# A fused attention and MLP kernel on one core: batch 0's set-up rebuilt, batch 1's inputs moved to GpSimd's DMA queue behind the weights

## The chip, the core and the metric

The kernel runs on one core of a Trainium2 chip. The metric is device time in microseconds (us). A core has a matrix engine (TensorE, PE in the profile), three other compute engines (VectorE or DVE, ScalarE or ACT, GpSimd or POOL) and SyncE (SP), which here only issues DMAs. Each engine executes its own instructions in program order and waits on semaphores for the others. PSUM is the memory that TensorE writes its results to.

Kernels sent in one call ran on the same chip and share the runs of the kernel before. The kernel before moved a little from call to call (medians 418.96 to 421.70 us), so between calls the ratios are compared, not the medians. A ratio is the mean time of one kernel's fast runs over that of the kernel before in the same rounds, so it is not quite the ratio of the quoted medians. Its 95% interval stands in brackets.

## The reference

Eight batches pass through windowed attention with eight global tokens, and then through a two-part MLP:

```python
# q, k, v: (8 batches, 8 heads, 576, 64); x after attention: (8, 576, 512)
scores = q @ k.T / 8, masked to |i-j| <= 32 or a global row or column (8 global tokens)
x   = softmax(scores) @ v
a1  = alpha1 * x + beta1
u   = x + lam * (w_tok @ a1)              # token mixing, w_tok is 576 x 576
ch  = relu((alpha2 * u + beta2) @ w_ch1) @ w_ch2     # 512 -> 2048 -> 512
out = u + lam * ch
```

## The kernel before

Names that return below: XL holds the scaled attention output that token mixing reads, UT the transposed u that the MLP reads, KTz a batch's transposed keys, wtT the transposed token weights, W1 and W2 the two MLP weights (each loaded in four blocks).

The rows of all batches are joined into nine MLP groups of 512 rows. While the MLP of one group runs, its matmuls are dealt out as "fillers" between the attention steps of the next batch, so that TensorE always has something to do. Batch 0 has no such partner, and batch 1 has only group 0.

```python
for _ in range(8): next(fill)             # fill yields after every MLP matmul
for b in range(1, NB):
    gen = front(b, kqn)                   # attention and mixing of batch b
    while True:
        try: n = next(gen)
        except StopIteration as s_: kqn = s_.value; break
        for _ in range(n): next(fill)
    done[0] = b + 1 if b < NB - 1 else 9  # groups below done[0] may run
for _ in fill: pass
```

For batches 0 and 1 the keys and queries are transposed on TensorE; batch 1's during batch 0's attention and mixing. From batch 2 on, `front(b)` loads the next batch's keys and queries on SyncE, casts them on GpSimd, and transposes them by DMA:

```python
# in front(b), when there is a batch b+1
cq = [qk_chunk(b + 1, c) for c in range(3)]         # loads on SyncE
kq, vg = gathers(b + 1)
yield from pg(b); yield from qk(b, 0)
for c in range(2): cq.pop(0)(G)                     # casts on GpSimd
for p in range(4):
    ...                                             # scores, global part
    pv(b, p, x)               # its last steps on GpSimd: XL[par] = x * (alpha1 * lam)
    if p == 0:   cq.pop(0)(G); cq = [qk_chunk(b + 1, c) for c in (3, 4)]
    elif p == 1: cq.pop(0)(G); cq.pop(0)(G)
    elif p == 2:
        kqn = glob_kq(kq)
        for c in range(5): xbar_k(c)                # DMA transposes on SyncE
        xbar_q()
        cv = [v_part(b + 1, i) for i in range(3)]   # V loads on SyncE
    else: ...                                       # V casts, shifts, global rows
yield 22
mix = tokmix(b, x)            # UT[g] = transpose of u*alpha2, by DMA on SyncE for b > 0
```

Each block of four output columns needs a bias row, which VectorE copies out of PSUM before ScalarE can apply relu:

```python
def mlp(g):
    for ec in range(16):
        if g == 0 and ec % 4 == 0: bias1(ec // 4)   # matmuls, then V.tensor_copy(bias1T)
        ps = ml()                                   # one of three PSUM buffers
        ... 4 matmuls into ps ...
        SC.activation(out=HTb[...], in_=ps, func=AF.Relu, bias=bias1T[:, ec:ec+1])
```

Batch 1's loads, and the issue of the weights, in program order (cut):

```python
n_k0 = qk4_half(1, 0, 0, next_r()); ...       # batch 1's k, q: SyncE, right after batch 0's
...
pv(0, 2, x); w1_dma(0); ...                   # W1 in four blocks on GpSimd
pv(0, 3, x); w1_dma(1); ...; w1_dma(2); w1_dma(3)
mix = tokmix(0, x) ...                        # batch 1's last key transposes in between
V.tensor_tensor(out=XL[1][0:1, 0, :], in0=b1r[0:1, :], in1=lamb[0:1, :], op=ALU.mult)
c_v = [v_part(1, i) for i in range(3)]        # batch 1's V: SyncE
for c in c_v: c(G)
v_shift(G)
for blk in range(4): w2_dma(blk)
```

The softmax here doesn't subtract the row's maximum and nothing guards it: scores larger than these inputs give would overflow.

## Time and profile before

The median of three runs was 417.88 us (417.57 to 422.43).

| event in the trace of before | us from start |
|---|---|
| first scores of batch 0 | 16.05 |
| first product with V (PV) | 22.8 |
| token mixing of batch 0 starts | 41.41 |
| first MLP matmul | 52.57 |
| second phase of MLP group 0 | 75.0 |
| token mixing of batch 1 | 87.3 |
| MLP group 1 starts | 108.20 |

From the page of the kernel before, these are the busy share of TensorE, its granted clock (10 tenths is printed as 9) and the DMA share, in forty slices of 10.4 us each, and then the chain that ended last:

```profile
PE   1665698969599999999999999999999999999995
PEclk9989999999699999999999999999999999999998
DMA  8996999999877999898999899899971003202001
PE 72%; DMA 12%; POOL 5%; DVE 4%; SPq 3%; issue 3%; ACT 1%; POOLq 0%; DVEq 0%
```

TensorE is full from the twelfth slice on. Only the first eleven slices, some 114 us, hold slack; the change is aimed at them. Each row of the next table is a stretch of the span (to the first MLP matmul, and from there to MLP group 1): length, then busy us of each engine, granted clock, DMA share and GB/s.

```profile
0.00:52.57 52.57, 28.91 (x393) 22.05 (x395) 36.97 (x92) 33.31 (x61) 32.34 (x51) 0.97 0.98 207
52.57:108.20 55.63, 45.40 (x435) 24.60 (x443) 29.63 (x61) 16.57 (x31) 31.05 (x40) 0.94 1.10 202
```

In the first stretch TensorE is busy 28.9 of 52.6 us, and in the second 45.4 of 55.6. TensorE's waits in the second stretch, as "who waited for whom: us in total, times, longest", are nearly two alone:

```profile
PE ml L482 <- DMA UT<-u_1502: 5.0, 1, 5.0
PE sc L401 <- POOL XL_116 L365: 3.2, 1, 3.2
```

### The profile page before, as it was taken

To read this page: it belongs to the slowest core of one execution; us is meant where nothing else is said; L and a number is where in the kernel's file an instruction comes from. 1 tells how busy PE (TensorE), PEld (TensorE's weight loads), DVE (VectorE), ACT (ScalarE), POOL (GpSimd) and SP (SyncE) were. 2 spreads that over 40 slices of the span, in tenths; PEclk is the share of its full clock that TensorE was granted. 3 is DMA by queue.
4 is the path that set the end of the run, shared out by engine and by line. 5 is a ranking of instruction groups with operands and counts; after the bars stand their busy time and mean duration, and the time that the engine had idled before them with its cause. 6 is when DMAs were issued, how large, how long until landed. Compare 5 with 4: busy or idle time off the path is not lost.

```text
span 415.1 us, 8399 instructions
## 1 busy us (share of the span) xinstructions
PE 372.6 (90%) x3349; PEld 206.5 (50%) x3403; DVE 227.2 (55%) x458; ACT 172.4 (42%) x303; POOL 181.1 (44%) x241
## 2 busy tenths in 40 slices
PE   1665698969599999999999999999999999999995
PEld 1554355524266456545654664466446644444442
DVE  6955843647246775575558753966374548114022
ACT  6848466300284047305730573047306720540720
POOL 7657354474445366754655473837440330000000
PEclk9989999999699999999999999999999999999998
DMA  8996999999877999898999899899971003202001
GB/s 235 224 301 105 171 218 193 210 161 244 190 138 115 194 219 215 148 209 186 212 151 206 196 211 170 175 222 192 166 178 53 2 27 85 56 0 77 25 25 76
DMA packets 174282, 64.14 MB, mean 155 GB/s; under 512 B 158498, under 2 KB 168226, under 8 KB 174244
## 3 DMA queue, kind: packets, MB, share of 16 engines
q1 hardware_dynamic: 167524, 54.63, 64.1%
q0 software_dynamic: 6720, 8.98, 11.7%
q8 instruction: 26, 0.43, 0.4%
q14 instruction: 12, 0.10, 0.1%
HBM read 39.28 MB, written 9.44 MB: 117 GB/s over the span
## 4 chain that ended last, share of the span: by engine, by line
PE 72%; DMA 12%; POOL 5%; DVE 4%; SPq 3%; issue 3%; ACT 1%; POOLq 0%; DVEq 0%
PE ml L491 26%; PE ml L482 26%; PE sc L405 6%; DMA vg<-in_v_dram,hg_idx 4%; PE xps L347 4%; DMA R_96<-in_v_dram 3%; PE sc L285 3%; PE xps L348 2%; DMA HTb<-in_moe_w_tok_dram 2%; PE mm L313 2%; SPq L203 1%; PE sc L330 1%; PE sc L401 1%; DMA RV_99<-in_v_dram 1%; POOL XL_116 L359 1%
## 5 line engine op out<-in xcount | busy, mean ns | idle before, releaser
L482 PE MATMUL ml<-UT,W_118 128*128 128x512 bf16 x542 | 141.0, 382 | 7.0 <-DMA UT<-u_1502 5.0
L491 PE MATMUL ml<-W_119,HTb 128*128 128x512 bf16 x561 | 135.2, 381 | 1.0 <-DMA W_119<-in_moe_w_ch_dram 0.2
L485 ACT ACTIVATE HTb<-ml,bias1T 128x512 bf16<-128x512 f32 x144 | 98.8, 688 | 87.8 <-PE ml L482 71.4
L491 PEld LDWEIGHTS <-HTb 128*128 128x128 bf16 x576 | 54.3, 98 | 61.3 <-issue 3.1
L482 PEld LDWEIGHTS <-W_118 128*128 128x128 bf16 x576 | 49.2, 99 | 45.9 <-issue 6.7
L496 DVE TENSOR_TENSOR tmp<-ml,lamb 128x512 f32<-128x512 f32 x36 | 24.8, 690 | 66.9 <-PE ml L491 50.8
L292 ACT ACTIVATE Pt<-sc 128x432 f16<-128x432 f32 x90 | 47.3, 528 | 14.2 <-PE sc L285 13.0
L285 PEld LDWEIGHTS <-KTz 128*128 128x128 bf16 x576 | 31.4, 102 | 21.3 <-PE mm L232 1.1
L359 POOL TENSOR_TENSOR XL_116<-x,LA_133 128x512 bf16<-128x512 f32 x16 | 20.8, 1300 | 32.6 <-DVE x L352 32.6
L285 PE MATMUL sc<-QT,KTz 128*128 128x72 bf16 x540 | 32.9, 200 | 1.1 <-DVE QT L235 0.8
L359 POOL TENSOR_TENSOR XL_115<-x,LA_133 128x512 bf16<-128x512 f32 x16 | 21.4, 1335 | 24.2 <-DVE x L352 23.2
L497 DVE TENSOR_TENSOR U<-tmp,U 128x512 f32<-128x512 f32 x36 | 29.5, 818 | 1.2
L406 DVE TENSOR_TENSOR U<-sc,x 128x512 f32<-128x512 f32 (+1 forms) x36 | 24.7, 687 | 9.1 <-PE sc L405 8.8
L331 ACT ACTIVATE GS_110<-sc 64x320 f16<-64x320 f32 (+1 forms) x8 | 3.2, 404 | 58.5 <-PE sc L330 58.2
L352 DVE TENSOR_TENSOR x<-xps,rden 128x640 f32<-128x640 f32 x32 | 26.4, 825 | 1.6
L331 ACT ACTIVATE GS_111<-sc 64x320 f16<-64x320 f32 (+1 forms) x8 | 3.2, 402 | 49.7 <-PE sc L330 49.7
L110 POOL CAST ve<-RV_98 128x1024 f16<-128x1024 f32 x8 | 10.0, 1244 | 31.4 <-DMA RV_98<-in_v_dram 31.3
L405 PE MATMUL sc<-XL_115,wtT_121 128*128 128x512 bf16 x79 | 19.7, 379 | 0.4 <-DVE U L406 0.3
L405 PE MATMUL sc<-XL_116,wtT_122 128*128 128x512 bf16 x76 | 19.7, 384 | 0.1
L294 DVE TENSOR_TENSOR GRT_108<-Pt,grm 128x80 f16<-128x80 f16 x16 | 4.3, 266 | 26.4 <-ACT Pt L292 26.4
L348 PE MATMUL xps<-RS_112,GS_110 128*128 128x65 f16 x160 | 15.9, 197 | 2.3 <-DVE RS_112 L321 2.3
L347 PEld LDWEIGHTS <-PTz_106 128*128 128x128 f16 x288 | 15.0, 97 | 5.8 <-DMA vo<-ve 1.6
(191 smaller groups left out, 525.1 us busy)
## 6 DMA issues: line engine op xcount, KB each, us to landing
out_dram<-U SPq DMA_DIRECT2D x36, 256.0 KB, 2.8
RV_99<-in_v_dram SPq DMA_DIRECT2D x16, 256.0 KB, 5.1
vo<-ve POOLq DMA_DIRECT2D x14, 260.0 KB, 4.1
R_97<-in_k_dram SPq DMA_DIRECT2D x12, 256.0 KB, 4.4
R_97<-in_q_dram SPq DMA_DIRECT2D x12, 256.0 KB, 5.3
RV_98<-in_v_dram SPq DMA_DIRECT2D x8, 256.0 KB, 3.9
W_118<-in_moe_w_ch_dram POOLq DMA_DIRECT2D x4, 512.0 KB, 8.9
W_119<-in_moe_w_ch_dram POOLq DMA_DIRECT2D x4, 512.0 KB, 13.7
```

Of the source, the lines that this page charges most:

```text
L285: T.matmul(out=ps[:, i * 144 + 72 * hh : i * 144 + 72 * hh + 72], lhsT=KTz[:, 2 * p + hh, 64 * t : 64 * t + P], rhs=A(QT, qo(t) + 80 * p, ...
L292: SC.activation(out=Pt[:, 432 * un : 432 * un + 432], in_=ps[:, 0:432], func=AF.Exp, bias=0.0, scale=0.125)
L347: T.matmul(out=o_, lhsT=ptz[:, base : base + P], rhs=vv, start=(i == 0), stop=False)
L352: V.tensor_tensor(out=A(x, P * p, [[64, 2], [DM, 5], [1, 64]]), in0=A(xps, 0, [[512, 2], [65, 5], [1, 64]]), in1=A(rden, 0, [[5, 2], [1, 5 ...
L359: G.tensor_tensor(out=A(xl, DM * full + P * p, [[DM, 4], [1, P]]), in0=A(x, DM * full + P * p, [[DM, 4], [1, P]]), in1=A(LA1, P * p, [[0, ...
L405: T.matmul(out=ps, lhsT=wtT[par][:, c, P * u : P * u + P], rhs=XL[par][:, c, :], start=(c == 0), stop=(c == 4))
L406: V.tensor_tensor(out=U[f][r0:r1, :], in0=ps[r0:r1, :], in1=x[r0:r1, u, :], op=ALU.add)
L482: T.matmul(out=ps, lhsT=W1[:, cc, ec * P : (ec + 1) * P], rhs=ut[:, cc, :], start=(cc == 0), stop=(cc == 3))
L485: SC.activation(out=HTb[:, slots[ec], :], in_=ps, func=AF.Relu, bias=bias1T[:, ec : ec + 1], scale=1.0)
L491: T.matmul(out=ps, lhsT=HTb[:, slots[ec], P * j : P * j + P], rhs=W2[:, ec, :], start=(ec == 0), stop=(ec == 15))
L496: V.tensor_tensor(out=tmp, in0=ps, in1=lamb, op=ALU.mult)
L497: V.tensor_tensor(out=u, in0=tmp, in1=u, op=ALU.add)
```

## The change

The intent is to shorten batch 0's start and to have every transfer arrive in the order in which it is needed. Core of the diff, with cuts:

```diff
-    def qk4_half(...) / qk4_rest(...)          # 4 heads per load, fixed to SyncE
+    def kq_load(E, b, i, h0, nh, r, off): ...   # any number of heads, engine E issues
+    onehot = cp.tile([P, 6, 8], BF16)           # global columns: keys x one-hot on TensorE
-    kq, vg = gathers(0)  ... gathers(1)         # for batches 0 and 1: indirect loads of k, q
+    vg = gather_v(0)     ... gather_v(1)        # only V is still gathered
+    def qk0_mm(p): ...                          # batch 0 scores on 64-row operands (XL[1] as buffer)
+    def v_half(hf, v4): ...                     # V of batch 0 in two halves; vo by copies
-    cq.pop(0)(G)                                # first two casts of batch b+1, for b >= 1
+    if cq and b > 1: cq.pop(0)(G)
-                if p == 0: ...  elif p == 1: ...  elif p == 2: ...  else: ...
+                late = b == 1                   # batch 2's casts and transposes one or two
+                if p == 2 * late: ...           # head pairs later than in other batches
+                elif p == 1 + 2 * late: ...
+                if p == 2 + late: ...           # DMA transposes, then V loads
+    wt_dma(0, 256); wt_dma(2, 256); wt_dma(4, 64); w1_dma(0)
     ... products with V of batch 0; w1_dma(1) between them ...
+    m3 = pv_mm(0, 3)
+    wt_tr(0); wt_tr(1)                          # token weights transposed after the last PV
+    w1_dma(2); w1_dma(3)
+    n_k = [kq_load(G, 1, 0, 4 * i, 4, R[i], 0) for i in range(2)]    # batch 1 on GpSimd
+    n_q = [kq_load(G, 1, 1, 0, 4, R[2], 0)]
+    n_rest = kq_rest(G, 1, u_tile())
+    n_q += [kq_load(G, 1, 1, 4 + 2 * i, 2, ub[i], 0) for i in range(2)]
+    c_v = [v_part(1, i, G, u_tile() if i == 2 else None) for i in range(3)]
     ... wt_tr, wt_sum ...
+    drain(tokmix(0, x))
+    G.memset(KTz, 0.0)                          # KTz no longer used by batch 0
+    G.memset(wtT[1][:, :, 0:64], 0.0); G.memset(wtT[1][0:64, 0, 64:640], 0.0)
+    for blk in range(2): w2_dma(blk)
+    G.memset(XL[1][0:64, 0, :], 0.0)            # XL[1] free only after batch 0's scores
     V.tensor_tensor(out=XL[1][0:1, 0, :], in0=b1r[0:1, :], in1=lamb[0:1, :], op=ALU.mult)
+    fillers(40)                                 # 40 MLP matmuls, then batch 1's transposes
+    for p in range(4): ... kt(1, p, V); fillers(3); qt(p, SC); fillers(3) ...
+    for blk in range(2, 4): w2_dma(blk)
     ...
-            for _ in range(n): next(fill)
+            fillers(n if b > 1 or used[0] < 64 else {4: 3, 5: 2, 6: 4, 10: 10}.get(n, 0))
```

## The prediction

> **What bounds the kernel now.** From about 112 us on the tensor engine (PE): its waits there sum to 1.1 us. Before that it is badly fed: the table by 5-us stretches shows 76 us of PE busy time in the first 110 us, so 34 us idle, and a granted clock of 0.66-0.67 at 25-30 and 90-95 us and 0.52 at 105-110 us. Only this part is changed. Landmarks in the timeline: scores of batch 0 begin at 16.05 us, PV at 22.8, token mixing at 41.4, the first MLP matmul at 52.6, MLP group 1 at 108.2. Large waits: 6.3 us for the first cast, 3.2 for XL at 87.7, 5.0 for the transposed u at 103.2. The chain of waits runs here through DMA: token weights (8.1 us), V of batch 1 (14.1), the V gather (14.6). Batch 1's q/k load from 19 us, ahead of W1, which is issued only at 37-43 us.
>
> **What the change does.**
> - Smaller first loads; no 2.19-us KTz memset and 2.33-us ScalarE copy before the first cast; batch 0's keys leave by one 128-row copy (about 0.7 us) instead of two 64-row ones (1.4 us).
> - One-hot columns remove k/q gathers (1 us of GpSimd each, plus landing) for batches 0 and 1, and add 80 small matmuls, at an estimated 0.06 us 2.4 us per batch.
> - V halves with on-chip shifts remove the vo transfer (4.5 us landing).
> - Batch 1 loads after the weights. The Trainium skill ("DMA: Bandwidth & Descriptors", Issuing engines are not separate DMA queues) says all queues share the same 16 engines; the trace agrees in that W1 blocks took 8.9 us (median) beside other loads. So order should help.
> - Batch 1's transposes move into MLP group 0; its attention gets fewer fillers (43 instead of 120), leaving 21 for batch 2.
>
> **On the critical path.** Estimates, from the new order with measured durations: scores near 10 us, PV near 20, XL complete near 32, mixing near 34, first MLP matmul 43-45. VectorE sets the pace (about 25 us of work before mixing, 8.4 us during it). That saves 8-9 us. From there to group 1 PE has about 47 us of work, including 4 us of moved transposes and one-hot products; I expect 5-9 us idle. The equivalent of group 1's start comes at 97-102 us instead of 108.2, and a re-throttle or two goes: the skill ("TensorE: Matmul & The Clock Gate", What's actually happening) says an idle window of about 3.4 us halves the clock; the trace has 0.52 around the 5.0-us wait. Net gain 6-15 us, centre 11.
>
> **Predicted: 407 us, 80% range 397 to 414. Faster by over 2%: 0.66; within 2%: 0.32; slower by over 2%: 0.02.**
>
> **What would show it.** First MLP matmul at 42-46 us; no 5-us wait for UT; PE idle in the first 100 us down by about 10 us; W1 block 0 landed before 40 us; batch 1's q/k/v landed by about 55 us.
>
> **What would make it wrong.** Smaller gain: GpSimd blocks on many small-row loads and a large KTz memset, so batch 1's keys come late; W2 blocks 2-3 late behind batch 1; three batch-2 casts ahead of batch 1's last XL product starve mixing by 3 us or more; VectorE sets batch 1's pace and the fewer fillers don't cover it. Larger gain: VectorE and DMA overlap better; the clock never drops from 40 to 110 us.

## The result and the profile after

The changed kernel took 442.19 us (440.75 to 444.42, four runs); the kernel before, beside it, 418.96 us (four runs). The ratio is 1.0546 [1.0462, 1.0630]: slower by 5.5%, where the centre of the prediction was faster.

| event | before, us | predicted, us | after, us |
|---|---|---|---|
| first scores | 16.05 | near 10 | 9.28 |
| first PV | 22.8 | near 20 | 24.0 |
| last XL product of batch 0 | | near 32 | 36.9 |
| token mixing starts | 41.41 | near 34 | 41.41 |
| first MLP matmul | 52.57 | 43 to 45 | 50.87 |
| as much left as at group 1 of before | 108.2 | 97 to 102 | 132.5 |

The last row is the span after, 439.3 us, less the 306.9 us that before still needed from its group 1 on (from the unrounded spans, 439.334 and 415.061 us). After's own group 1 starts at 134.50 us and needs 304.8 us. So nothing was lost behind group 1; the loss of 24.2 us between the two profiled spans lies ahead of it, and batch 0 even gave 1.7 us. The same rows of the page, after (slices of 11.0 us):

```profile
PE   3568728775967999999999999999999999999995
PEclk9985869999796999999999999999999999999999
DMA  7878999603999988998999898869995002301101
PE 70%; DVE 10%; DMA 7%; POOL 6%; SPq 3%; issue 3%; ACT 1%; DVEq 0%; POOLq 0%; ACTq 0%
```

Two things are new: the clock is lowest in the fourth and sixth slices, and the DMA engines are nearly idle in the ninth. The stretches after, cut at the first MLP matmul, the end of its long stall, batch 1's first attention matmul, its token mixing and group 1:

```profile
0.00:50.87 50.87, 31.03 (x409) 23.08 (x411) 36.76 (x95) 17.86 (x41) 34.49 (x50) 0.86 0.83 183
50.87:63.90 13.03, 4.07 (x12) 1.52 (x12) 0.75 (x2) 0.74 (x2) 11.17 (x11) 0.63 0.93 185
63.90:86.70 22.80, 17.96 (x174) 9.78 (x175) 10.70 (x25) 12.24 (x23) 7.05 (x8) 0.92 0.97 176
86.70:105.67 18.97, 15.45 (x256) 10.74 (x261) 14.73 (x32) 6.63 (x14) 7.95 (x9) 1.00 0.01 3
105.67:134.50 28.83, 18.87 (x99) 8.35 (x100) 12.77 (x21) 2.93 (x6) 14.12 (x21) 0.85 1.04 190
```

In the second row TensorE is busy for 4.1 of 13 us and VectorE and ScalarE for less than 1 each, while GpSimd is busy for 11.2. In the fourth row DMA moves 3 GB/s, and in the fifth it is full.

**The stall of 8.7 us.** GpSimd's timeline there, as "start, duration, engine, line, operation, what it writes and reads, count", with the idle time just before and what ended it in brackets:

```profile
46.42 0.83 POOL L209 DMA_DIRECT2D RV<-in_v_dram  x1 [3.07 <-DMA W<-in_moe_w_ch_dram]
48.64 0.90 POOL L209 DMA_DIRECT2D RV<-in_v_dram  x1 [1.39 <-DMA R<-in_k_dram]
50.90 0.88 POOL L209 DMA_DIRECT2D RV<-in_v_dram  x1 [1.37 <-DMA R<-in_k_dram]
53.28 0.88 POOL L209 DMA_DIRECT2D RV<-in_v_dram  x1 [1.50 <-DMA R<-in_q_dram]
...
55.10 4.38 POOL L813 MEMSET KTz<- 128x5120 bf16 x1
...
61.73 0.56 POOL L818 MEMSET XL<- 64x512 bf16 x1
```

A V load writes a free buffer and reads an input, so its data give it nothing to wait for. Yet each waits for another DMA to land. The operands in the trace show why: GpSimd's DMAs signal on eight completion semaphores, numbered 111 to 118, in turn, and each first waits until the DMA that had its semaphore before, the eighth back, has landed. The first V load waits on 118, which W1's last block had signalled; the next three wait on 111, 112 and 113, which belong to batch 1's two key loads and its first query load. These are exactly the releasers in the brackets, and the same count fits e1, e2, e5, e9 and e14 below. After four such waits (7.3 us) come the clear of KTz, two clears of wtT, two W2 issues, and only then the small clear of XL. VectorE, ScalarE and TensorE stood in line behind it:

```profile
62.33 0.68 DVE L823 TENSOR_TENSOR XL<-U,lamb 1x512 bf16<-1x512 f32 x1 [11.50 <-POOL XL L818]
62.94 0.14 DVE L579 COPY bias1T<-mm 128x4 f32<-128x4 f32 x1
63.16 1.84 ACT L557 ACTIVATE HTb<-ml,bias1T 128x512 bf16<-128x512 f32 x3 [21.27 <-DVE bias1T L579]
63.90 1.44 PE L554 MATMUL ml<-UT,W 128*128 128x512 bf16 x3 [8.73 <-ACT HTb L557]
```

VectorE writes one row of XL (L823), which needs the clear. It stands ahead of the bias copy, and VectorE runs in order. The relu lacks its bias, no PSUM buffer comes free, and TensorE, which could fill three, stops. The XL row itself is used more than 40 us later, in the mixing of batch 1 (105.67 us).

The Trainium skill ("TensorE: Matmul & The Clock Gate", What's actually happening) says that after an idle window of about 3.4 us TensorE falls back to half clock. The trace agrees: the wait lasted from 55.17 to 63.90 us; at its end, from 60 to 64 us, the granted clock was 0.50, and it was still 0.54 from 64 to 68 us.

**The end of batch 1.** The waits between 104 and 136 us:

```profile
DVE u L481 <- DMA UT<-u: 8.2, 1, 8.2
PE ml L554 <- DMA UT<-u: 6.4, 1, 6.4
PE sc L470 <- POOL XL L434: 3.5, 1, 3.5
```

GpSimd made six casts for batch 2 (104.37 to 107.76 us) ahead of batch 1's last XL product (107.73), and mixing waited 3.5 us for it. On SyncE, the UT transposes (L485) came last:

```profile
108.34 7.26 SPq L194 DMA_TRANSPOSE KTz<-kz  x5
115.70 1.34 SPq L197 DMA_TRANSPOSE QT<-q  x1
117.13 2.42 SPq L198 DMA_TRANSPOSE QT<-q  x1
119.65 3.48 SPq L209 DMA_DIRECT2D RV<-in_v_dram  x4
...
124.64 2.50 SPq L485 DMA_TRANSPOSE UT<-u  x2
127.86 5.43 SPq L485 DMA_TRANSPOSE UT<-u  x3
```

VectorE writes u into three buffers. With none transposed before 124.64 us it stopped, and MLP group 1 waited for the late transposes. Before, the first UT transpose was issued at 98.67 us, about 8 us after mixing resumed; after, some 15 us. The change did not create this queue; `late` moved the transposes for batch 2 from the idle ninth slice to just ahead of those for UT.

### The profile page after: what moved, and what is told of

Read it like the earlier page. It is cut to its first block, busy times and chain, and to the rows that moved or that the text cites. A ratio compares the mean times of both kernels' runs of the same rounds, so it can differ in the third digit from the quotient of the medians.

```text
span 439.3 us, 8613 instructions
## 1 busy us (share of the span) xinstructions
PE 384.8 (88%) x3441; PEld 212.8 (48%) x3496; DVE 239.4 (54%) x481; ACT 162.7 (37%) x291; POOL 193.2 (44%) x247
## 4 chain that ended last, share of the span: by engine, by line
PE 70%; DVE 10%; DMA 7%; POOL 6%; SPq 3%; issue 3%; ACT 1%; DVEq 0%; POOLq 0%; ACTq 0%
PE ml L554 27%; PE ml L563 24%; DMA R<-in_q_dram 5%; PE sc L474 5%; PE sc L328 3%; PE xps L400 3%; DMA UT<-u 2%; PE mm L359 2%; PE xps L401 2%; PE sc L376 2%; POOL XL L428 1%; POOL KTz L813 1%; SPq L209 1%; DVE x L421 1%; DVE PTz L346 1%
## 5 line engine op out<-in xcount | busy, mean ns | idle before, releaser
L554 PE MATMUL ml<-UT,W 128*128 128x512 bf16 x545 | 140.9, 389 | 17.2 <-ACT HTb L557 8.7
L563 PE MATMUL ml<-W,HTb 128*128 128x512 bf16 x556 | 137.4, 381 | 1.0
L554 PEld LDWEIGHTS <-W 128*128 128x128 bf16 x576 | 51.3, 100 | 63.6 <-issue 13.9
L428 POOL TENSOR_TENSOR XL<-x,LA 128x512 bf16<-128x512 f32 x31 | 40.8, 1317 | 70.2 <-DVE x L421 69.9
L474 PE MATMUL sc<-XL,wtT 128*128 128x512 bf16 x156 | 41.2, 394 | 0.3 <-issue 0.2
L481 DVE TENSOR_TENSOR u<-U,a2b 128x512 bf16<-128x512 f32 x36 | 30.1, 837 | 9.4 <-DMA UT<-u 8.2
L400 PEld LDWEIGHTS <-PTz 128*128 128x128 f16 x576 | 30.7, 99 | 9.5 <-issue 4.0
L400 PE MATMUL xps<-ve,PTz 128*128 128x65 f16 x300 | 30.4, 194 | 1.2 <-DVE x L421 1.0
L401 PE MATMUL xps<-RS,GS 128*128 128x65 f16 x300 | 29.3, 194 | 2.3 <-DVE RS L367 2.2
L328 PE MATMUL sc<-QT,KTz 128*128 128x72 bf16 x504 | 29.8, 199 | 0.6 <-ACT Pt L335 0.4
L401 PEld LDWEIGHTS <-GS 128*128 128x128 f16 x320 | 28.5, 99 | 2.4 <-issue 1.0
L340 DVE TENSOR_TENSOR GRT<-Pt,grm 128x80 f16<-128x80 f16 x32 | 13.0, 407 | 29.8 <-ACT Pt L335 29.7
```

Source lines behind the costliest of these rows:

```text
L328: T.matmul(out=ps[:, i * 144 + 72 * hh : i * 144 + 72 * hh + 72], lhsT=KTz[:, 2 * p + hh, 64 * t : 64 * t + P], rhs=A(QT, qo(t) + 80 * p, ...
L400: T.matmul(out=o_, lhsT=ptz[:, base : base + P], rhs=vv, start=(i == 0), stop=False)
L401: T.matmul(out=o_, lhsT=gs[:, P * u : P * u + P], rhs=rs[:, h, :], start=False, stop=True)
L428: E.tensor_tensor(out=A(xl, DM * full + P * p, [[DM, 4], [1, P]]), in0=A(x, DM * full + P * p, [[DM, 4], [1, P]]), in1=A(LA1, P * p, [[0, ...
L474: T.matmul(out=ps, lhsT=wtT[par][:, c, P * u : P * u + P], rhs=XL[par][:, c, :], start=(c == 0), stop=(c == 4))
L481: V.tensor_tensor(out=u16, in0=U[f], in1=a2b, op=ALU.mult)
```

## The experiments

The theories (the expectations name them by letter or by content). **A**: GpSimd is held (by its waits for earlier DMAs and by clears), and through XL's clear it holds VectorE, ScalarE and TensorE; this is the larger loss. **B**, the rival: the order of transfers in the one queue is at fault, with batch 1's data late behind the weights. **C**: the late placement of batch 2's work costs the 3.5 and 6.4 us at the end of batch 1. **D**: GpSimd's casts in batch 0 slow VectorE, and that keeps mixing at 41 us.

### One part at a time

**e1**: clear XL's rows ahead of the last W1 blocks and batch 1's loads.

```diff
     pv_norm(0, 3, x, m3, V)
+    G.memset(XL[1][0:64, 0, :], 0.0)
     w1_dma(2)
...
-    G.memset(XL[1][0:64, 0, :], 0.0)
```

> Changed kernel, with one thing moved: the 0.56-us clearing of 64 rows of the batch-1 tile XL on GpSimd goes ahead of the last two W1 loads and all batch-1 loads. Theory A (GpSimd is held at the batch-1 V loads because only eight of its DMAs may be under way, the clearing stands behind them, VectorE waits for it with the bias copies of the MLP behind that): the 8.7-us wait of the MLP at 55.2 to 63.9 us goes, batch 1's first attention matmul comes near 76-78 us instead of 86.7, total 442 to 430-435 us. Rival B (the batch-1 data itself comes too late in the one queue, so PE would only wait at the next place): the wait moves to the first key transpose or the KTz copy and the total stays above 438 us.

Measured: 435.84 us, ratio 1.0372 [1.0330, 1.0414]. The 8.7-us wait is gone, and the second MLP phase starts at 81.95 us instead of 87.26. The total lies between the two forecasts (430 to 435, and above 438). GpSimd is held as long as before, and TensorE now meets two waits of 2.42 and 2.64 us for batch 1's casts on VectorE. These casts were not waiting for data; they were slow. The first, 128x1024 at 56.85 us, ran beside GpSimd's clear of KTz (55.09 to 59.47) and took 3.99 us, where the same cast took 0.68 at 72.05 us in this trace. The second, at 62.83 us, took 1.70, beside GpSimd's DMA issues. So the clear of XL was the link to TensorE, but only part of the loss; GpSimd's clear of KTz costs time a second way. No run changes that clear alone.

**e2**: batch 2's work where the other batches have it.

```diff
-                late = b == 1
+                late = False
```

> Changed kernel, with batch 2's casts, transposes and loads put back to the same places in batch 1's attention as in every later batch (they had been moved two head pairs later). Theory C (the late placement leaves the DMA idle from 84 to 105 us, then puts the casts ahead of batch 1's last XL product and the transposes of u behind everything): the 3.5-us wait for XL at 105.7 shrinks to under 2 us, the 6.4-us wait for the transposed u at 128 shrinks to under 2 us, total 442 to 432-437 us. Rival (these waits are covered or replaced by others, PE then waits for batch 2's keys instead): total within 3 us of 442.

Measured: 435.30 us, ratio 1.0348 [1.0305, 1.0391]. The wait for UT is gone. The wait for XL is not; it grew to 4.5 us, because casts still stand ahead of the product. The MLP stall came to 10.9 us in this profile, as the MLP began 1.7 us sooner and the clear came no earlier. C holds for UT; for XL its cure was wrong.

**e3**: all of batch 1's loads issued by SyncE, in the same places of the program. **e5**: only the five V loads, so that keys and queries stay behind the weights in GpSimd's queue.

```diff
 e3 and e5
-    c_v = [v_part(1, i, G, u_tile() if i == 2 else None) for i in range(3)]
+    c_v = [v_part(1, i, nc.sync, u_tile() if i == 2 else None) for i in range(3)]
 e3 alone
-    n_k = [kq_load(G, 1, 0, 4 * i, 4, R[i], 0) for i in range(2)]      # also n_q, n_rest
+    n_k = [kq_load(nc.sync, 1, 0, 4 * i, 4, R[i], 0) for i in range(2)]
```

> Changed kernel, with all batch-1 q, k, v loads issued by SyncE (hardware queue) instead of GpSimd, same program order otherwise, so they start when their buffers are free, from about 18-25 us, beside the weights. Theory A: GpSimd is no longer held, KTz is cleared by about 43-45 us, the 8.7-us MLP wait goes, as in the run with the clearing first, and the key transposes are not late: 428-436 us; W1 then lands later than before but still in time. Rival B' (order in one queue is what matters, mixing delays the weights): W_tok and W1 land late, token mixing or the MLP waits for weights, total at or above 440 us.

> Changed kernel, with only the five batch-1 V loads on SyncE; k and q stay behind the weights in GpSimd's queue. Theory A (what costs is that GpSimd itself is held at the V loads, not the order of the queue): GpSimd no longer waits between 43 and 55 us, KTz and XL are cleared by about 50 us, the 8.7-us MLP wait goes, total as in the run with everything on SyncE, 428-433 us. Rival B (the order, with k and q behind the weights, is what costs): the 8.7-us wait goes but waits for late k and q of batch 1 replace it, total 434-438 us, as in the run with only the clearing moved.

Measured: e3 430.14 us, ratio 1.0228 [1.0172, 1.0284]; e5 430.04 us, ratio 1.0220 [1.0196, 1.0244]. They are the same. Where the keys and queries stand does not matter here; five V loads do. In e5, GpSimd went on 12 us sooner:

```profile
43.06 4.38 POOL L813 MEMSET KTz<- 128x5120 bf16 x1
...
49.70 0.56 POOL L818 MEMSET XL<- 64x512 bf16 x1
...
53.40 0.76 POOL L592 DMA_DIRECT2D W<-in_moe_w_ch_dram  x1 [1.55 <-DMA R<-in_q_dram]
54.44 0.74 POOL L592 DMA_DIRECT2D W<-in_moe_w_ch_dram  x1 [0.28 <-DMA U<-in_k_dram]
```

The last two lines test the count of eight. With the V loads gone, W2's third block has the query load as its eighth predecessor, and the fourth block the key rest; these are what they waited for. The second MLP phase began at 75.42 us in e5 and 74.68 in e3. B falls; A stands.

**e4**: batch 0's casts of the later heads on ScalarE instead of GpSimd.

```diff
-    c_q23(G)
+    c_q23(SC)
...
-    c_k47(G)
-    c_q47(G)
+    c_k47(SC)
+    c_q47(SC)
```

> Changed kernel, with the three batch-0 casts of q/k (q of heads 2-3, k and q of heads 4-7) on ScalarE, which is half idle there, instead of GpSimd. Theory D (VectorE small operations of 0.2 us took about 1.0 us at 12-15 us[...], and this ate the gain in batch 0): those operations return to 0.2 us, token mixing starts 2-3 us before 41.4 us. But the 8.7-us wait later hangs on GpSimd's DMA queue, which starts from the weights issued after the V casts, so the total gains only 1-3 us (439-441). Rival (batch 0 is held by something else, such as GpSimd's XL products or ScalarE): token mixing still starts at 41-42 us and total within 1 us of 442.

Measured: 442.75 us, ratio 1.0544 [1.0502, 1.0586], no change. The part of D about instruction lengths is right. In the kernel after, GpSimd casts ran from 12.08 to 13.35 us and from 13.64 to 14.68, and beside them two VectorE operations on very small tiles read:

```profile
12.37 1.06 DVE L279 TENSOR_TENSOR U<-U 128x72 f32<-128x72 f32 x1
13.70 1.02 DVE L281 TENSOR_TENSOR grm<-U,notg 128x40 f16<-128x40 f32 x1
```

In the kernel before the same two read:

```profile
13.23 0.23 DVE L251 TENSOR_TENSOR U<-U 128x72 f32<-128x72 f32 x1
13.72 0.20 DVE L253 TENSOR_TENSOR grm<-U,notg 128x40 f16<-128x40 f32 x1
```

The Trainium skill ("SBUF — State Buffer", Who interferes with whom) says that a VectorE instruction with two inputs in SBUF contends with a GpSimd instruction that reads SBUF. Both operations have two such inputs, and they took 1.06 and 1.02 us against 0.23 and 0.20 in before, where GpSimd was idle then; in e4 they took 0.23 and 0.20 again. So the trace agrees. VectorE's busy time before mixing fell from 29.8 us in after to 27.2 in e4. But the time does not pay. In e4's profile mixing began at 37.72 us, the stall grew to 11.8 us and ended at 62.3 us, about where it ended before. That profile also had the full clock at 28 to 44 us, where after had 0.50 at 32 to 40, so not even the 3.7 us by which mixing began sooner can be put down to the casts.

### Do the parts add up?

**e6** is e2 and e3 together; **e7** adds e4's casts; **e8** adds to e7 that batch 1's casts run during the first 40 MLP matmuls and that batch 1's last XL product is made on VectorE.

```diff
 e8, besides the edits of e2, e3 and e4
-            pv(b, p, x)
+            pv_norm(b, p, x, pv_mm(b, p), V if b == 1 and p == 3 else G)
...
-    fillers(40)
+    for c in (n_k[0], n_q[0], n_rest, n_k[1], n_q[1], n_q[2]):
+        fillers(8 if c is n_k[0] else 0)
+        c(V)
+    fillers(32)
     for p in range(4):
-        if p % 2 == 0: n_k[p // 2](V)        # and n_q, n_rest in the same way
         kt(1, p, V)
```

> Both repairs at once: batch-1 loads on SyncE, and batch 2's casts and loads at their early places. If the two losses are separate (theory A and theory C each right): 430 minus about 7 = 421-425 us. If they share one cause, or one only moves the other's wait: 427-430 us.

> As the kernel with both repairs, and the three batch-0 casts on ScalarE. That move alone let token mixing begin 3.7 us earlier and the total did not follow, because the MLP wait ended at a time set by GpSimd. With that wait gone the earlier start should now reach the end: 2.5-4.5 us under the kernel with both repairs. If batch 0's start is not on the path even now: within 1 us of it.

> As the kernel before it, plus: batch 1's q/k casts on VectorE are put ahead of the key copies, during the first 40 MLP matmuls when VectorE is idle, and batch 1's last XL product goes to VectorE instead of standing behind batch-2 casts on GpSimd. PE's waits of 1.6, 0.9 and 1.3 us at the key transposes and the 3.5-4.5 us wait for XL should go: 4-8 us under the kernel before it, 410-416 us, which would be below the original kernel (420.4 in the earlier rounds). If VectorE merely shifts the waits to the key copies and score masks: under 3 us.

Measured: e6 425.13 us, ratio 1.0114 [1.0082, 1.0146]; e7 425.18 us, ratio 1.0115 [1.0084, 1.0147]; e8 419.84 us, ratio 0.9967 [0.9939, 0.9994]. From the ratios, e3 takes off 0.032 and e2 0.020; together that would be 0.052, and e6 took 0.043. The two parts nearly add, so they are separate losses. Of e6's waits the largest left is

```profile
PE sc L470 <- POOL XL L434: 4.5, 1, 4.5
```

so bringing batch 2 forward removes the UT wait and makes the XL wait slightly longer. e7 again gives nothing for the casts, where 2.5 to 4.5 us were forecast; but its mixing began at 41.36 us (40.01 in e6), so the earlier start seen in e4 was not there, and e7 does not test what such a start is worth. e8 missed its forecast of 410 to 416 us, but brings the changed kernel level with before: the casts in the idle time of VectorE and the XL product were worth 1.5%, though on VectorE, with GpSimd casts beside it, that product took 2.69 us (0.88 for batch 0's last one on VectorE in after), the XL wait was still 2.4 us, and a wait of 3.7 us for UT came back.

### Can the one queue be repaired?

**e9** keeps every load on the queue that the change gave it and repairs only the holding: XL cleared early (as e1), KTz cleared by VectorE before mixing, batch 0's casts on ScalarE, batch 1's casts at once after the 40 fillers, batch 2 early with its first two casts where before had them, and batch 2's V loads ahead of its DMA transposes. **e10** is e9 with batch 1's loads on SyncE. **e11** is e9 with the casts back on GpSimd.

```diff
 e9
-            if cq and b > 1:
+            if cq:
                 cq.pop(0)(G)
-                late = b == 1
+                late = False
+                    if b == 1: cv = [v_part(b + 1, i) for i in range(3)]   # ahead of xbar_k
+    G.memset(XL[1][0:64, 0, :], 0.0)          # before w1_dma(2)
+    V.memset(KTz, 0.0)                        # before drain(tokmix(0, x))
-    G.memset(KTz, 0.0)
     fillers(40)
+    for c in (n_k[0], n_q[0], n_rest, n_k[1], n_q[1], n_q[2]):
+        c(V)
 ...                                          (cut: the lines removed for these, and e4's edit)
```

> Changed kernel with its one queue in order of need kept, and everything taken out from behind it or put right around it: XL cleared before the loads, KTz cleared by VectorE while it waits for the token weights, batch-0 casts on ScalarE, batch 1's casts ahead of the key copies but after the first 40 MLP matmuls, batch 2's casts and loads at their early places including the two casts before the first head pair, V loads of batch 2 ahead of its transposes. If the order of need is worth something once GpSimd's wait holds up nobody: token mixing near 38 us, no wait over 3 us afterwards, 408-415 us, below the original's 421. If the order itself is of no use: 418-422.

> The same repairs, but batch 1's loads on SyncE from about 18 us, beside the weights. If order of need helps (the token weights come later beside batch 1's loads, as in the run with both repairs and ScalarE casts, where mixing began at 41.4 instead of 37.7): 3-5 us above the one-queue version. If what made mixing late there was GpSimd's KTz clearing beside VectorE: within 1 us of it, or below because batch 1's data are there sooner.

> The one-queue repaired kernel with batch 0's three casts left on GpSimd, as the change has them. If batch 0's start is on the path now: 2.5-4.5 us above it, with token mixing 3 us later. If not: within 1 us.

Measured, with five rounds: e9 419.72 us, ratio 1.0004 [0.9969, 1.0040]; e10 416.77 us, ratio 0.9909 [0.9883, 0.9935]; e11 419.62 us, ratio 0.9983 [0.9964, 1.0002]. So the whole loss of 5.5% goes without touching the one-queue idea: what cost the time was mostly what stood in line with the queue, not the queue's order. (Mostly, as the early casts of batch 1 are an addition and not an undoing.) But the queue is no gain either: e9 was forecast at 408 to 415 us, with mixing near 38, if the order is worth something; mixing began at 41.20 us and the time lies in the rival's 418 to 422. Batch 1's loads on SyncE are 3 us better (e10 against e9). With batch 0's casts on ScalarE or GpSimd (e9, e11) mixing began at 41.20 and 41.07 us and the time is the same, so D does not explain the late mixing in this kernel. Whether the casts would matter once the token weights come early (e12 and e13 below have them on ScalarE) was not run.

The clear of KTz on VectorE appears in e9 as

```profile
37.38 2.19 DVE L816 MEMSET KTz<- 128x2560 uint32 x1 [0.19 <-issue]
```

against 4.38 us on GpSimd for the same bytes. The Trainium skill ("VectorE: DVE Perf Modes", Zero memsets can be issued as uint32 (trn2)) says that a VectorE clear of 2-byte elements can be issued at 4 bytes per element with half the elements. The trace shows the halved count: 2560 elements of uint32 instead of 5120, and half of GpSimd's time. Both clears took 0.86 ns for each element in a row (4.38 us by 5120, 2.19 by 2560). No run clears it on VectorE in 2-byte elements, so the page's comparison itself was not tested here.

### The rest of the missing gain: batch 0

In the kernel after, XL was complete at 36.9 us, but mixing began at 41.41. Between lay the transposes and sums of the token weights on TensorE, all after the last PV, from 33.94 to 41.4 us at a granted clock of 0.50. **e12** is e10, with the token weights issued 5.7 us earlier (16.70 us against 22.45; four small clears on GpSimd that they need move ahead with them, not shown) and two of their five transposes and sums placed between the products with V. **e13** is e9 with the same edit. **e14** is the changed kernel with that edit alone.

```diff
+    wt_dma(0, 256); wt_dma(2, 256); wt_dma(4, 64)     # before glob_v, xg(0, 0)
-    wt_dma(0, 256); wt_dma(2, 256); wt_dma(4, 64)     # after vo_half(V, 1)
     w1_dma(1)
+    wt_tr(0)
     xg(0, 2)
...
+    wt_tr(1); wt_sum(0)
     xg(0, 3)
+    wt_sum(1)
     m3 = pv_mm(0, 3)
-    wt_tr(0); wt_tr(1)
```

> The repaired kernel with batch 1 on SyncE (416.8), plus: the token weights are issued on GpSimd about 5 us earlier (after the casts of the first V half instead of after the second), and two of the five weight transposes and two of the five sums run on PE between batch 0's PV products instead of after them. Theory E (batch 0's rebuilt start gains nothing because 7 us of weight transposes and sums wait behind the last PV, at half clock[...]): token mixing begins 2-4 us before 41.5, total 412.5-415. Rival F (VectorE's chain to the last XL product, which ended near 36.8, sets mixing; the rest only fills): mixing at 40-41.5, total within 1.5 us of 416.8.

> The same addition on the repaired kernel with one queue (419.7). Theory E: mixing 2-4 us earlier, total 415-418. Rival F: within 1.5 us of 419.7.

> The changed kernel with this addition alone. Mixing begins 2-4 us earlier under theory E. The total should follow by under 2 us (440.5-442.5), because the MLP wait ends when GpSimd has cleared XL, and GpSimd reaches that at a time set by its loads, not by mixing: the 8.7-us wait should grow by what mixing gains. If the total falls by 3 us or more, the wait is not tied to GpSimd's loads.

Measured, with five rounds for e12 and e13 and three for e14: e12 414.14 us, ratio 0.9819 [0.9775, 0.9862]; e13 416.40 us, ratio 0.9882 [0.9833, 0.9931]; e14 441.86 us, ratio 1.0461 [1.0401, 1.0522]. Before was 421.70 us in that call. In e14 mixing began at 40.42 us, only 1.0 us sooner than after (2 to 4 were forecast), and the MLP at 49.76, 1.1 us sooner; the stall took it back.

```profile
49.76 2.75 PE L554 MATMUL ml<-UT,W 128*128 128x512 bf16 x11 [0.21 <-DVE UT L451]
63.31 1.87 PE L554 MATMUL ml<-UT,W 128*128 128x512 bf16 x4 [10.80 <-ACT HTb L557]
```

The stall's end, 63.31 us, is set by GpSimd and hardly moved from 63.90, and the second phase of group 0 came no sooner (89.50 us against 87.26). Once the stall is out of the way, the earlier start carries through: in e12 mixing began at 37.11 us (41.49 in e10), the MLP at 47.61 (50.06), the second phase at 71.24 (72.73) and group 1 at 108.87 (111.25). The ratios cannot tell the two cases apart: from e10 to e12 the ratio fell by 0.0090, from after to e14 by 0.0085 with overlapping intervals, and each pair comes from different calls. e12 is the best kernel and beats both. It is 1.8% faster than before, with an interval wholly below 1 but reaching across the 2% mark. In its page the slices of TensorE read

```profile
PE   2587798769899999999999999999999999999995
```

and its largest wait of TensorE between 40 and 140 us is 2.3 us in total, for u.

## Why the prediction was wrong

- **"Scores near 10 us": right**, 9.28.
- **"PV near 20, XL complete near 32, mixing near 34": wrong by 4, 5 and 7 us**, and the first MLP matmul came at 50.87 instead of 43 to 45. "VectorE sets the pace" did not hold to the end: after XL was complete, the weight transposes and sums on TensorE took 4.5 us more, at half clock. The prediction left 2 us between XL and mixing and names no clock. VectorE's own work was mis-sized too: it was busy for 29.8 us before mixing instead of about 25 (27.2 in e4, without GpSimd's casts beside it). e12 moved mixing to 37.1 us by taking two of the five transposes and sums away from there; but those left also ran at full clock (0.44 us for five against 0.72 to 0.74), so the edit and the clock are not separated.
- **The step that failed most: "From there to group 1 PE has about 47 us of work ...; I expect 5-9 us idle."** The equivalent of group 1 came 81.6 us after the first MLP matmul (132.5 less 50.87) instead of 52 to 56. Up to its own group 1 TensorE was busy for 56.4 us (the sum of the last four stretches shown of after) and idle for 27.3 of the 83.6. The idle time is the mis-sized term: the waits for the relu, XL, UT and batch 1's casts are 8.7, 3.5, 6.4 and 3.8 us, 22.4 in all. With what causes them repaired, e9 is level with before (1.0004). The busy time was longer too, with the granted clock low around the long waits (mean 0.63 in 50.87 to 63.90 us and 0.85 in 105.67 to 134.50 us).
- **The risk was named but its path was not.** "GpSimd blocks on many small-row loads and a large KTz memset" was listed as a smaller gain, by late keys. The runs showed both parts true: waits of 7.3 us and a clear of 4.38 us. But they reached TensorE through an unrelated small clear, one row on VectorE and the bias copies behind it. e5 took this away by moving five loads, and the ratio fell from 1.0546 to 1.0220. A chance of 0.02 for slower was far too small when the risks listed added up to a loss.
- **"No 5-us wait for UT": wrong**, it was 6.4 us. The diff shows `late`, and I did not follow what stood ahead of UT's transposes on SyncE. The risk of "3 us or more" for XL was right, at 3.5 us.
- **"So order should help": not borne out.** e10 and e12, with batch 1 on SyncE, are 3.0 and 2.3 us faster than e9 and e13. The Trainium skill ("DMA: Bandwidth & Descriptors", Issuing engines are not separate DMA queues) says that issuing on several engines saves only the sequencer's time, usually small. The issue itself was indeed small here: 0.79 to 0.90 us for each V load, against 7.5 to 11.8 us until it landed. But with 7.3 us of waits for earlier DMAs the five issues held GpSimd from 43 to 55 us, and moving them took the ratio from 1.0546 to 1.0220. Of the landing times, "W1 block 0 landed before 40 us" was right (about 34.3), and "batch 1's q/k/v landed by about 55 us" held for keys and queries but not for V (about 61.8).
- **"PE idle in the first 100 us down by about 10 us": wrong.** Idle time was 28.9 us before and 36.4 after (100 less 71.10 and 63.60 busy).

What stays open: why the granted clock was 0.50 at 32 to 36 us in most of these kernels, and 1.00 through 32 to 40 us in e4 and e13, as in before. Runs of the same kernel may differ there, and one profile of each cannot tell. That e9 loses 3 us to e10 was measured, but not traced to one wait: in the profiles 2.0 of the 2.2 us between them at group 1 arise between the first MLP matmul and the second phase, where e9 waits 2.1 us for copies to KTz and the granted clock at 50 to 70 us was 0.91 against 1.00.

## What to carry to other kernels

An issue of a DMA is an instruction of its engine and can wait like any other: before moving loads to an engine that also computes, count how many will be under way, and look at everything that follows them in that engine's order. A small operation that is needed only much later can stop the whole core if it stands early on an in-order engine and depends on a late one; place such clears before the loads. And when a later stage waits for something else, ask what ends that wait before working on an earlier stage: in e4 the MLP began 4.8 us sooner than in after and the stall still ended at 62.3 us, set by GpSimd, so the time did not change; with the stall gone, the profile of e12 still shows 2.4 us of its earlier start at group 1.

## What the Trainium skill lacked or had wrong

- "DMA: Bandwidth & Descriptors", Issuing engines are not separate DMA queues: "usually small" holds for the issue itself (0.79 to 0.90 us against 7.5 to 11.8 us to land), but the section does not say that the issuing engine can be held. In this program, whose GpSimd DMAs use eight completion semaphores in turn, four V loads on GpSimd waited 3.07, 1.39, 1.37 and 1.50 us for the DMA eight before them. No page that I found states such a wait.
- "VectorE: DVE Perf Modes", Zero memsets can be issued as uint32 (trn2): the halved count was seen, but no run clears on VectorE in 2-byte elements. No page that I found sets GpSimd beside it: the same bytes took 4.38 us on GpSimd as 5120 bf16 elements and 2.19 us on VectorE as 2560 uint32 elements, 0.86 ns for each element on both.
- "SBUF — State Buffer", Who interferes with whom: it agreed (1.06 against 0.23 us for a two-input operation), but e4 and e7, and e9 against e11, gained nothing from avoiding it. A larger case is in e1: a one-input cast beside GpSimd's clear took 3.99 us against 0.68, and TensorE waited for it.
- "TensorE: Matmul & The Clock Gate", What's actually happening: it agreed around the 8.7-us wait (0.50 granted at its end, from 60 to 64 us). It did not let me foresee 0.50 at 32 to 40 us, where TensorE was busy for 6.2 of 8 us (2.75 and 3.41 us in the two halves).
